# A Fourier filter and a SiLU feed-forward network in one kernel: the first token pairs in two runs, weight rounding moved into the steps, and sums of the inverse transform on GpSimd

## The chip, the cores and the metric

The kernel runs on one core of one Trainium2 chip. The metric is the device time in microseconds (us) of that core; before the change it is 2591.91, the median of 3 runs (2589.95 to 2593.28).

The engines are named as the profile names them: PE is TensorE (matmuls; PEld its weight loads), DVE is VectorE, ACT is ScalarE, POOL is GpSimd, SP is SyncE, which here only issues DMAs. A name with a q (SPq) is an engine's instruction queue.

## What is computed

Two stages follow each other. The first filters every channel of a sequence in the frequency domain; the second is a two-layer network on every token:

```python
# x: (8, 3008, 256); filt_r, filt_i: (1505, 256)
X = np.fft.rfft(x, axis=1)
Y = X * (filt_r + 1j * filt_i)[None]
y = np.fft.irfft(Y, n=3008, axis=1).astype(np.float32)
# 8 * 3008 = 24064 tokens of 256; w_in: (256, 2048), w_out: (2048, 256), both float64
t = y.reshape(24064, 256)
h = t @ w_in
g = h * (1.0 / (1.0 + np.exp(-h)))
out = (g @ w_out).astype(np.float32)
```

## The kernel before

**The transform.** 3008 = 47 x 64, so a transform is done in matmuls with small tables. Stage 1 (tiles `pa`) works along one factor, `forward` (`pb`, L433) along the other. `multiply` (L455) takes the products with the filter, `z` with its real and `p` with its imaginary part. `add` (L463) sums them to a complex product. The inverse is in two parts: `pc` (L476, or L498 for batch 0), whose rows are written to a scratch tensor `d` in HBM, and stage 3 (`pd`, L547), which reads them back as `t4` tiles. Its result is evicted to `y`, half a batch at a time. The 24 slots of frequencies are handled in six groups.

**Batch 0 has a path of its own,** since nothing can hide it: `load_first`, `stage1_first`, `inverse_first`, `rows_first`. `inverse_first` of groups 0 and 1 (`by_gpsimd`) multiplies the sums that GpSimd made. For groups 2 to 5 no sums are made: PE takes twice as many matmuls, with negated tables `neg`. Stage 1 of batch 0 writes into `w_t`, the place where the weights lie later. The transforms of batches 1 to 7 are cut into pieces that lie between FFN matmuls.

**The FFN.** Weights and tokens are cut in 2 x 2, and each product is made with 7 instead of 8 block products (Winograd's form of Strassen's scheme). A *pair* is a set of 2 x 256 tokens (2 x 240 for each third one) of half a batch; there are 48 pairs. A *step* is one pair with one of NJP = 8 pairs of weight blocks: `hidden` has seven matmuls into `px` and `pyz` (L689), sums of them on DVE, SiLU on ACT and four differences on DVE; `project` (L752) has seven matmuls into the accumulators `acc`, one step later. A step has 8 rounds, in which these two and the other pieces take turns. After the eight steps of a pair, `drain` copies the accumulators to `s`, GpSimd makes seven sums and `output` transposes and stores. There is one `s` buffer and one buffer for each accumulator. `tokens` makes the three sums of tokens that a pair needs (`ty`).

**The weights.** They are float64, 16 blocks (j = 0 to 15). A block is rounded to float32 from its two 32-bit words. In `split_weights`, DVE takes exponent and mantissa apart (L877, L880) and ACT converts them (L879, L881). In `round_weights`, DVE adds the low word (L893), limits the exponent (L895) and puts the sign in (L899). In `place_weights` (L908) mantissa and exponent are multiplied into `w_t`. `combine_weights` makes the sums that the scheme needs, for two blocks together. Before the change blocks 0 to 8 are rounded ahead of the FFN, 9 to 15 one a step in steps 0 to 6, where a block's split and rounding stand at one place (round 1) and its placing at round 5.

**Order.** The schedule is written by hand: every engine executes in the order in which the program names the instructions, and semaphores do the rest. Pieces in the FFN are put at a step and a round with `put`. `idle(n)` are matmuls without a use ahead of a stretch of work. DMA issues of SP and ACT stand in their engines' order: an issue that waits holds up all that is behind it.

Of the kernel before, what the change touches and what calls it, by code (L numbers as in the profile page):

```python
# [56 lines left out]
NS, NG = 24, 6  # L57
# [110 lines left out]
def kernel(  # L168
# [96 lines left out]
    def spectral(b):  # L265
# [12 lines left out]
        def load_first():  # L278


            view = w_t.rearrange("p j c w n -> p (j c w n)")
            for at, n0, n in ((view[:, 0:3072], 0, 12), (view[:, 3072:6144], 12, 12),
                              (x_all.rearrange("p i a n -> p (i a n)"), 24, 8)):
                nc.sync.dma_start(out=at, in_=bass.AP(tensor=x.tensor, offset=x.offset + n0 * C,
                                                      ap=[[32 * C, 128], [1, n * C]]))
            xs[0] = view[:, 0:6144].rearrange("p (n c) -> p n c", c=C)
            xs[1] = x_all.rearrange("p i a n -> p (i a n)").rearrange("p (n c) -> p n c", c=C)
            us["t2"] = view[:, 6144:14336].rearrange("p (s c) -> p s c", c=C)
            return view

        def stage1_first(k, i):

            if i == 0:
                banks[k] = bank(b, f"pa_{b}_{k}").rearrange("p a c -> p (a c)").rearrange(
                    "p (n c) -> p n c", c=16)
            n0, n = ((0, 24), (24, 8))[i]
            nc.tensor.matmul(out=banks[k][:, n0:n0 + n], lhsT=wx_t, rhs=xs[i][0:96, :, 16 * k:16 * k + 16],
                             start=True, stop=True)
            if i == 1:
                nc.vector.transpose(out=us["t2"][:, :, 16 * k:16 * k + 16].rearrange("p s c -> p c s"),  # L300
                                    in_=banks.pop(k).rearrange("p n c -> p c n"))
# [139 lines left out]
        def multiply(g, k):  # L441
            if b == 0 and g == NG - 1:

                room = raws["first"].bitcast(FP32).rearrange("p (k i r c) -> p k i r c", k=2, i=2, r=2)
                z, pt = room[:, k, 0], room[:, k, 1]
            else:
                z = zpool.tile([128, 2, C], FP32, name=f"z_{b}_{g}_{k}", tag="z")
            if b == 0 and g == NG - 1:
                pass
            elif b == 0 and k == 1:  # L450
                pt = abcpool.tile([128, 3, C], FP32, name=f"p_{b}_{g}_{k}", tag="abc")[:, 0:2]
            else:
                pt = ppool.tile([128, 2, C], FP32, name=f"p_{b}_{g}_{k}", tag="p")
# [6 lines left out]
        def add(g, k):  # L460
            z, pt = prods[g][k]
            eng = nc.vector if b > 0 else nc.gpsimd
# [19 lines left out]
        def inverse_first(g):  # L482
# [3 lines left out]
            pairs = prods.pop(g)  # L486
            halves[g] = ps
            for h in range(2):
                table = e_t[:, g] if h == 0 else minus[g // 4][:, g % 4]
                terms = [(table[:, :, 0], 0, 0), (table[:, :, 1], 0, 1)]  # L490
                if g not in by_gpsimd:
                    terms += [(table[:, :, 1], 1, 0), (neg[h][:, g], 1, 1)]
                for t, (lhs, which, ri) in enumerate(terms):
                    for i in range(2):
                        rows = slice(64 * i, 64 * i + 64)
                        for k in range(2):

                            nc.tensor.matmul(out=ps[i][64 * k:64 * k + 64, h, :], lhsT=lhs[rows, k],  # L498
                                             rhs=pairs[k][which][rows, ri, :], start=(h == 0 and t == 0),
                                             stop=(t == len(terms) - 1), skip_group_check=True)  # L500

        def rows_first(g):
            for i, pool, tag in ((0, qpool, "q"), (1, opool, "o")):
                qt = pool.tile([128, 2, C], FP32, name=f"q_{b}_{g}_{i}", tag=tag)
                nc.scalar.copy(out=qt, in_=halves[g][i])
                a0 = 8 * g + 4 * i
                queue = nc.gpsimd if g == NG - 2 else nc.scalar
                queue.dma_start(out=d2[a0:a0 + 4].rearrange("a n h c -> (a n) h c"), in_=qt)
# [17 lines left out]
        def load_t4(g, first=0, last=2 * NS):  # L526
# [4 lines left out]
            for h in range(2):  # L531
                queue = nc.scalar if first == 32 and h == 1 else nc.sync
# [125 lines left out]

    def combine(eng, out, in0, in1, op):
# [6 lines left out]
    def tokens(pair):  # L666

        n, yt = pairs[pair][3], channels(pair)
        t = typool.tile([128, 4, CH], FP32, name=f"ty_{pair}", tag="ty")
# [4 lines left out]
        ty[pair] = t  # L674

    def hidden(step):

        pair, jp = divmod(step, NJP)
        n, yt, t = pairs[pair][3], channels(pair), ty[pair]
# [55 lines left out]
    def project(step):  # L735

        pair, jp = divmod(step, NJP)
        n, g = pairs[pair][3], g_t.pop(step)
        if jp == 0:
            acc[pair] = {}  # L740
        last = jp == NJP - 1

        order = PROJECT
        if jp == 0 and step in joined:
            order = PROJECT[0:2] + PROJECT[3:5] + PROJECT[2:3] + PROJECT[5:]
        elif jp == 0:
            order = PROJECT[2:3] + PROJECT[0:2] + PROJECT[3:]
        for c, k, i, h in order:
            if i not in acc[pair]:
                acc[pair][i] = accps.tile([128, 2, 256], FP32, name=f"acc_{pair}_{i}", tag=f"a{i}")  # L750

            nc.tensor.matmul(out=acc[pair][i][:, h, 0:n], lhsT=w_t[:, jp, c, 1], rhs=g[:, k, 0:n],  # L752
                             start=(jp == 0 and h == 0), stop=last, skip_group_check=True)
            if last and (h == 1 or i == 3):
                drain(pair, i)
            yield

    results = {}

    def drain(pair, i):  # L760
        n = pairs[pair][3]

        if i == 0:
            results[pair] = spool.tile([128, 8, CH], FP32, name=f"s_{pair}", tag="s")
# [3 lines left out]
        if pair == len(pairs) - 1:  # L768
            return drain_last(pair, i, n, s, acc[pair])
        copy = v.tensor_copy if i % 2 else nc.scalar.copy  # L770
        if i < 3:
            copy(out=s[:, 2 * i:2 * i + 2, 0:n], in_=acc[pair][i][:, :, 0:n])  # L772
            return
        copy(out=s[:, 6, 0:n], in_=acc.pop(pair)[3][:, 0, 0:n])
        for o, a, b in ((2, 0, 2), (5, 0, 5), (3, 5, 3), (6, 3, 6), (0, 5, 1), (4, 0, 4), (1, 3, 1)):
            combine(gp, s[:, o, 0:n], s[:, a, 0:n], s[:, b, 0:n], ALU.add)
# [20 lines left out]
    def output(pair, chunk):  # L797
# [3 lines left out]
        for h in range(2):  # L801
            v.transpose(out=o[:, :, h, :], in_=results[pair][:, ((2, 6), (4, 1))[chunk][h], :])
# [34 lines left out]
    def load_weights(j):  # L837

        if j in (8, 11, 12, 13):
            pool, tag = (t4pool, "t4") if j in (11, 12) else (upool, "u")  # L840
            raw = pool.tile([128, 2, 512], U32, name=f"raw_{j}", tag=tag)
        else:

            if j in (0, 2):
                t = ypool.tile([128, 2, HALF], FP32, name=f"raw_{j}", tag="y")
                raws.setdefault("tiles", []).append(t)
                raws["at"] = t.rearrange("p a n -> p (a n)").bitcast(U32)[:, 0:2048]
                raws["y"] = raws["at"]
                raws.setdefault("first", raws["at"])
            elif j == 4:  # L850
                raws["at"] = spool.tile([128, 2048], U32, name=f"raw_{j}", tag="s")
            elif j == 6:
                raws["at"] = gpool.tile([128, 2048], U32, name=f"raw_{j}", tag="g")
            elif j in (9, 14):
                raws["at"] = raws["y"]
            at = 1024 * (j in (1, 3, 5, 7, 10, 15))
# [7 lines left out]
    def split_weights(*js):  # L864

        for j in js:
            words = raws[j].rearrange("p w (n t) -> p (w n) t", t=2)
            if j < 8:
                if "scratch" not in raws:
                    raws["scratch"] = gpool.tile([128, 4, 512], U32, name="scratch", tag="g")  # L870
                e, m = (raws["scratch"][:, 2 * (j % 2) + i] for i in range(2))
            else:
                e = zpool.tile([128, 512], U32, name=f"e_{j}", tag="z")
                m = ppool.tile([128, 512], U32, name=f"m_{j}", tag="p")
            raws[j] = lo, hi, e, m, ef, mf = (words[:, :, 0], words[:, :, 1], e, m, e.bitcast(FP32),
                                              m.bitcast(FP32))
# [263 lines left out]
```

## Time and profile before

| | |
|---|---|
| time | 2591.91 us |
| span of the profile | 2589.2 us |
| first FFN matmul | 80.54 us |
| second step begins | 89.35 us |
| mean TensorE clock | 0.996 of full |

A line of a timeline has the start, the length, the engine, the source line, the operation, output <- inputs, shapes and the count; in brackets is the idle time before it and what ended it. A line of a table by stretches has the stretch, its length, then the busy time (and count) of PE, PEld, DVE, ACT and POOL, the granted clock of PE (1.00 is full), the share of the DMA engines and GB/s. On the page, section 1 has busy time, share and instructions of each engine, and section 4 the shares of the chain of waits that ended last. Instructions overlap in an engine's pipeline, so that a distance from start to start is often shorter than a length.

### The profile page before, as it was taken

To read this page: it belongs to the slowest core of one execution; us is meant where nothing else is said; L and a number is where in the kernel's file an instruction comes from. 1 tells how busy PE (TensorE), PEld (TensorE's weight loads), DVE (VectorE), ACT (ScalarE), POOL (GpSimd) and SP (SyncE) were. 2 spreads that over 40 slices of the span, in tenths; PEclk is the share of its full clock that TensorE was granted. 3 is DMA by queue.
4 is the path that set the end of the run, shared out by engine and by line. 5 is a ranking of instruction groups with operands and counts; after the bars stand their busy time and mean duration, and the time that the engine had idled before them with its cause. 6 is when DMAs were issued, how large, how long until landed. Compare 5 with 4: busy or idle time off the path is not lost.

```text
span 2589.2 us, 48332 instructions
## 1 busy us (share of the span) xinstructions
PE 2567.9 (99%) x18972; PEld 2196.3 (85%) x18972; DVE 1691.3 (65%) x3569; ACT 1106.9 (43%) x3014; POOL 426.4 (16%) x672
## 2 busy tenths in 40 slices
PE   8999999999999999999999999999999999999998
PEld 6788888888888888888888888888888888888987
DVE  7766666666666766666666676666666676555554
ACT  3544444444444444443444434444444444444443
POOL 2211211121112111211122111211121112101101
PEclk9899999999999999999999999999999999999999
DMA  8431232222222222222223222231233211210000
GB/s 281 145 82 48 65 80 70 60 61 74 62 63 60 77 66 55 72 68 67 62 62 88 54 66 58 79 72 54 64 75 74 63 47 27 59 25 15 9 17 16
DMA packets 200076, 171.07 MB, mean 66 GB/s; under 512 B 122116, under 2 KB 174196, under 8 KB 199060
## 3 DMA queue, kind: packets, MB, share of 16 engines
q1 hardware_dynamic: 178520, 117.04, 18.7%
q0 software_dynamic: 16928, 44.65, 5.3%
q10 hardware_dynamic: 4400, 6.29, 0.8%
q8 instruction: 149, 2.44, 0.4%
q14 instruction: 79, 0.65, 0.1%
HBM read 96.05 MB, written 81.26 MB: 68 GB/s over the span
## 4 chain that ended last, share of the span: by engine, by line
PE 95%; DVE 1%; DMA 1%; ACT 1%; issue 0%; SPq 0%; ACTq 0%; DVEq 0%
PE acc L752 43%; PE px L689 26%; PE pyz L689 19%; PE pd L547 3%; PE pb L433 2%; PE pc L476 2%; PE pf L403 1%; PE pa L340 0%; DMA w_t<-in_x_dram 0%; DVE g L660 0%; PE pa L331 0%; DMA filt<-in_filt_i_dram 0%; ACT t L344 0%; DMA e_t<-e_tbl 0%; DVE w_t L660 0%
## 5 line engine op out<-in xcount | busy, mean ns | idle before, releaser
L752 PE MATMUL acc<-g,w_t 128*128 128x256 f32 (+1 forms) x5376 | 1512.0, 375 | 0.4 <-DVE g L660 0.4
L752 PEld LDWEIGHTS acc<-g,w_t 128*128 128x128 f32 x5376 | 1021.3, 190 | 115.7 <-DVE g L660 0.8
L660 DVE TENSOR_TENSOR g<-pyz,abc 128x256 f32<-128x256 f32 (+1 forms) x1152 | 479.7, 416 | 563.0 <-ACT abc L710 325.0
L660 DVE TENSOR_TENSOR g<-g 128x256 f32<-128x256 f32 (+3 forms) x1152 | 609.9, 529 | 196.9 <-ACT g L693 183.7
L689 PE MATMUL px<-ty,w_t 128*128 128x256 f32 (+1 forms) x2304 | 684.4, 379 | 0.5 <-ACT abc L710 0.5
L693 ACT ACTIVATE g<-g 128x256 f32<-128x256 f32 (+1 forms) x1152 | 472.9, 410 | 246.7 <-DVE g L660 246.7
L689 PEld LDWEIGHTS px<-ty,w_t 128*128 128x128 f32 x2304 | 426.3, 190 | 82.3 <-issue 26.6
L660 POOL TENSOR_TENSOR s<-s 128x256 f32<-128x256 f32 (+1 forms) x329 | 257.1, 799 | 1439.1 <-DVE s L772 1377.4
L689 PE MATMUL pyz<-y,w_t 128*128 128x256 f32 (+1 forms) x1536 | 452.9, 377 | 0.0
L689 PEld LDWEIGHTS pyz<-y,w_t 128*128 128x128 f32 x1536 | 284.3, 189 | 44.8 <-DVE g L660 5.0
L704 ACT COPY abc<-px 128x256 f32<-128x256 f32 (+1 forms) x384 | 141.5, 368 | 361.3 <-PE px L689 361.3
L710 ACT COPY abc<-px 128x256 f32<-128x256 f32 (+1 forms) x384 | 143.1, 373 | 323.7 <-PE px L689 323.7
L693 ACT ACTIVATE g<-px 128x256 f32<-128x256 f32 (+1 forms) x384 | 146.1, 381 | 308.6 <-PE px L689 308.6
L689 PE MATMUL px<-y,w_t 128*128 128x256 f32 (+1 forms) x768 | 230.2, 381 | 1.1 <-ACT y L246 1.0
L689 PE MATMUL pyz<-ty,w_t 128*128 128x256 f32 (+1 forms) x768 | 225.7, 376 | 0.2 <-DVE g L660 0.2
L689 PEld LDWEIGHTS px<-y,w_t 128*128 128x128 f32 x768 | 141.9, 189 | 23.6 <-issue 5.9
L689 PEld LDWEIGHTS pyz<-ty,w_t 128*128 128x128 f32 x768 | 145.9, 190 | 17.4 <-DVE g L660 1.0
L697 ACT COPY abc<-px 128x256 f32<-128x256 f32 (+1 forms) x384 | 135.5, 353 | 19.5 <-PE px L689 19.5
L547 PEld LDWEIGHTS pd<-wi_t,t 48*64 48x64 f32 x4096 | 69.3, 139 | 32.0 <-ACT g L693 16.4
L547 PE MATMUL pd<-wi_t,t 48*64 48x47 f32 x4096 | 77.2, 238 | 2.3 <-DMA t<-d 1.9
L415 POOL DMA_DIRECT2D d<-tf x144 | 71.4, 503 | 24.0 <-DVE tf L411 20.4
L772 ACT COPY s<-acc 128x512 f32<-128x512 f32 (+1 forms) x94 | 54.3, 578 | 47.5 <-PE acc L752 47.5
(114 smaller groups left out, 1309.1 us busy)
## 6 DMA issues: line engine op xcount, KB each, us to landing
t<-d SPq DMA_DIRECT2D x120, 192.0 KB
d<-q POOLq DMA_DIRECT2D x86, 256.0 KB, 2.6
t<-d SPq DMA_DIRECT2D x84, 256.0 KB
out_dram<-o SPq DMA_DIRECT2D x636, 32.0 KB
d<-tf POOLq DMA_DIRECT2D x144, 96.0 KB, 3.0
xr<-in_x_dram SPq DMA_DIRECT2D x6, 1472.0 KB
x_all<-in_x_dram SPq DMA_DIRECT2D x72, 96.0 KB
x_all<-xr SPq DMA_DIRECT2D x72, 96.0 KB
```

Of the source, the lines that this page charges most:

```text
L415: nc.gpsimd.dma_start(out=d1[k // 2, :, k % 2, n0:n0 + 4], in_=us["tf"][32 * k:32 * k + NS].rearrange("p q n c -> p (q n) c"))
L433: nc.tensor.matmul(out=ps[k][32 * j:32 * j + 32, ri, :], lhsT=d_t[rows, 4 * g + at, ri, :], rhs=t2[rows, at, :], start=True, stop=True)
L476: nc.tensor.matmul(out=ps[j][64 * k:64 * k + 64, a, :], lhsT=e_t[rows, g + a, k, ri, :], rhs=zs[k][rows, ri, :], start=(a == 0 and ri == 0 ...
L547: nc.tensor.matmul(out=ps[h][c0:c0 + 64, cb, i, :], lhsT=t4s[g][rows, i, 128 * cb + c0:128 * cb + c0 + 64], rhs=wi_t[rows, :], start=True, ...
L660: eng.tensor_tensor(out=out, in0=in0, in1=in1, op=op)
L689: nc.tensor.matmul(out=out, lhsT=w_t[:, jp, c, 0], rhs=rhs, start=start, stop=True, skip_group_check=True)
L693: nc.scalar.activation(out=g[:, k, 0:n], in_=g[:, k, 0:n] if src is None else src, func=AFT.Silu)
L697: nc.scalar.copy(out=sums[:, 0, 0:n], in_=xo)
L704: nc.scalar.copy(out=sums[:, 1, 0:n], in_=xo)
L710: nc.scalar.copy(out=sums[:, 2, 0:n], in_=xo)
L752: nc.tensor.matmul(out=acc[pair][i][:, h, 0:n], lhsT=w_t[:, jp, c, 1], rhs=g[:, k, 0:n], start=(jp == 0 and h == 0), stop=last, skip_group ...
L772: copy(out=s[:, 2 * i:2 * i + 2, 0:n], in_=acc[pair][i][:, :, 0:n])
```

## The change

It shortens what has to be done ahead of the first FFN step. Only four weight blocks (0 to 3) are rounded there. The first three pairs are therefore taken in two runs each: pair 0 with weight pairs 0 and 1, then pairs 1 and 2 with weight pairs 0 to 3, then the rest of all three. So new weight pairs are needed in steps 4, 5 and 12 to 15. The sums of a first run are kept (`partial`, in `upool` and in parts of `x_all`), and GpSimd adds them to those of the second. Blocks 4 to 15 are rounded in steps 0 to 3 and 5 to 12, with the four parts of a rounding in rounds 1, 2, 4 and 5 and the placing in round 6.

In the prologue, x comes in 96 instead of 128 partitions, with three matmuls for each transpose. All six groups have their products summed, by GpSimd, or by DVE for the second half of groups 4 and 5; the matmuls with `neg` go. The last eviction of `rows_first` is on DVE, ahead of which nothing else is left. ACT issues the last reads of two slabs instead of half of all.

```diff
-                nc.sync.dma_start(out=at, in_=bass.AP(tensor=x.tensor, offset=x.offset + n0 * C,
-                                                      ap=[[32 * C, 128], [1, n * C]]))
+                nc.sync.dma_start(out=at[0:96], in_=bass.AP(tensor=x.tensor, offset=x.offset + n0 * C,
+                                                            ap=[[32 * C, 96], [1, n * C]]))
...
         def multiply(g, k):
-            if b == 0 and g == NG - 1:
-                room = raws["first"].bitcast(FP32).rearrange("p (k i r c) -> p k i r c", k=2, i=2, r=2)
-                z, pt = room[:, k, 0], room[:, k, 1]
+            if b == 0 and g in (2, 3):
+                if "room" not in us:
+                    us["room"] = gpool.tile([128, 2, 2, 2, C], FP32, name="room", tag="g")
+                z = us["room"][:, g - 2, k]
...
-            eng = nc.vector if b > 0 else nc.gpsimd
+            eng = nc.vector if b > 0 or (g > 3 and k == 1) else nc.gpsimd
...
-                terms = [(table[:, :, 0], 0, 0), (table[:, :, 1], 0, 1)]
-                if g not in by_gpsimd:
-                    terms += [(table[:, :, 1], 1, 0), (neg[h][:, g], 1, 1)]
...
-                nc.scalar.copy(out=qt, in_=halves[g][i])
+                copy = nc.vector.tensor_copy if (g, i) == (NG - 1, 1) else nc.scalar.copy
+                copy(out=qt, in_=halves[g][i])
...
-                queue = nc.scalar if first == 32 and h == 1 else nc.sync
+                queue = nc.scalar if first == 32 and g > 1 else nc.sync
...
+    runs = [(0, 0, 2), (1, 0, 4), (2, 0, 4), (0, 2, 8), (1, 4, 8), (2, 4, 8)]
+    runs += [(pair, 0, NJP) for pair in range(3, len(pairs))]
+    schedule = [(run, jp) for run, (_, first, end) in enumerate(runs) for jp in range(first, end)]
...
     def drain(run, i):
...
+        kept = partial.pop(pair, None)
+        if end < NJP:
+            room = x_all[:, pair - 1] if pair else upool.tile([128, 2, 512], FP32, name="partial", tag="u")
+            partial[pair] = room.rearrange("p a (i n) -> p (a i) n", n=CH)
         for o, a, b in ((2, 0, 2), (5, 0, 5), (3, 5, 3), (6, 3, 6), (0, 5, 1), (4, 0, 4), (1, 3, 1)):
-            combine(gp, s[:, o, 0:n], s[:, a, 0:n], s[:, b, 0:n], ALU.add)
+            out = s[:, o, 0:n]
+            if end < NJP and o in FINAL:
+                out = partial[pair][:, FINAL.index(o), 0:n]
+            combine(gp, out, s[:, a, 0:n], s[:, b, 0:n], ALU.add)
+        if kept is not None:
+            for k, o in enumerate(FINAL):
+                combine(gp, s[:, o, 0:n], s[:, o, 0:n], kept[:, k, 0:n], ALU.add)
...
-    for g in range(2):
+    def inverse(g):
+        part["inverse_first"](g)
+        part["rows_first"](g)
+
+    for g in range(4):
         part["forward"](g)
     for g in range(NG):
         for k in range(2):
             part["multiply"](g, k)
-        if g in by_gpsimd:
-            for k in range(2):
-                part["add"](g, k)
...
-            split(2, 3)
-            rounded(2, 3)
-            placed(2, 3, eng=gp)
-            combine_weights(1, eng=gp)
...
+            part["add"](g, k)
+        if g == 3:
+            part["forward"](5)
+        if g > 0:
+            inverse(g - 1)
+        if g == 1:
+            part["forward"](4)
+        if g == 3:
             for later in range(4):
                 part["load_t4"](later, 0, 24)
...
-    split(4, 5)
-    combine_weights(0)
...
-    split(6, 7, 8)
...
+    inverse(NG - 1)
     for later in range(4):
+        part["load_t4"](later, 32, 2 * NS)
+    second["load_x"](0)
+    weights(4, 5)
+    second["load_x"](1)
+    for k in range(2):
+        for j in (2, 3):
+            round_weights(j, k)
     combine_weights(0)
+    for k in (2, 3):
+        for j in (2, 3):
+            round_weights(j, k)
+    placed(2, 3)
+    combine_weights(1, eng=gp)
+    weights(6, 7)
+    idle(30)
     for g in range(4):
         part["stage3"](g)
...
-    for j in range(9, NJ):
-        put(j - 9, 1, lambda j=j: (split(j), rounded(j)))
-        put(j - 9, 5, placed, j)
+    for j in range(4, NJ):
+        at = j - 4 if j < 8 else j - 3
+        for k, rnd in enumerate((1, 2, 4, 5)):
+            put(at, rnd, round_weights, j, k)
+        put(at, 6, placed, j)
         if j % 2:
+            for k, rnd in ((0, 3), (1, 5)):
+                put(at + 1, rnd, combine_weights, j // 2, k)
+    for step, *js in ((0, 8, 9), (4, 10, 11, 12, 13), (10, 14), (11, 15)):
+        put(step, 0, weights, *js)
+    joined.update((2, 6, 10, 20))
...
+    begun = ((-2, 1), (0, 5), (4, 5), (8, 5), (14, 5), (18, 5))
+    early_stores = (((18, 1), (18, 5)), ((22, 1), (22, 5)))
```

## The prediction

> **What bounds the kernel now.** I read the shares and the chain of waits first, then the PE timeline of the first 100 us, then the other engines beside it.
>
> ```profile
> PE 2567.9 (99%) x18972; PEld 2196.3 (85%) x18972; DVE 1691.3 (65%) x3569; ACT 1106.9 (43%) x3014; POOL 426.4 (16%) x672
> PE 95%; DVE 1%; DMA 1%; ACT 1%; issue 0%; SPq 0%; ACTq 0%; DVEq 0%
> ```
>
> TensorE (PE) is the bound: 99% busy and 95% of the chain. The change leaves the matmuls of the FFN as they are, so it can only move the moment at which the FFN starts, or put holes into it. The PE timeline shows that moment:
>
> ```profile
> 69.93 0.28 PE L547 MATMUL pd<-wi_t,t 48*64 48x47 f32 x2
> 72.10 6.76 PE L547 MATMUL pd<-wi_t,t 48*64 48x47 f32 x246 [1.89 <-DMA t<-d]
> 79.09 0.47 PE L547 MATMUL pd<-wi_t,t 48*64 48x47 f32 x8 [0.23 <-issue]
> 80.54 1.19 PE L689 MATMUL px<-y,w_t 128*128 128x256 f32 x2 [0.98 <-ACT y L246]
> ```
>
> The first FFN matmul is at 80.54; step 1 begins at 89.35. From there to 2589.2 PE waits for almost nothing. So the prologue, 80.5 us, is what can be won. Why it is so long stands in the VectorE (DVE) and GpSimd (POOL) timelines:
>
> ```profile
> 17.95 14.25 DVE L300 STREAM_TRANSPOSE w_t<-pa 128x512 f32<-128x512 f32 x16 [7.25 <-PE pa L297]
> 34.33 0.69 DVE L455 TENSOR_TENSOR z<-pb,filt 128x512 f32<-128x512 f32 x1 [0.89 <-PE pb L433]
> 35.77 0.73 POOL L463 TENSOR_TENSOR z<-z,p 128x256 f32<-128x256 f32 x1 [34.33 <-DVE p L455]
> 36.46 0.73 POOL L464 TENSOR_TENSOR z<-z,p 128x256 f32<-128x256 f32 x1
> 63.63 0.95 DVE L880 TENSOR_SCALAR scratch<-raw 128x512 uint32<-128x512 uint32 x1
> 63.46 3.44 POOL L660 TENSOR_TENSOR w_t<-w_t 128x256 f32<-128x256 f32 x4 [0.47 <-DVE w_t L908]
> ```
>
> Transposes run every 0.89 us, products of the filter every 0.60, GpSimd adds every 0.69. The weight rounding stands between the products on VectorE. The last two lines show a cost used below: a TENSOR_SCALAR that takes 0.42 us takes 0.95 while GpSimd adds.
>
> After 80.54 the balance of a step is in the table by stretches (PE, PEld, DVE, ACT, POOL busy):
>
> ```profile
> 107.90:115.80 7.90, 7.90 (x33) 5.88 (x32) 6.29 (x16) 4.42 (x11) 1.97 (x4) 1.00 0.36 104
> 143.50:149.60 6.10, 6.10 (x30) 5.22 (x29) 3.99 (x9) 2.90 (x10) 1.97 (x4) 1.00 0.43 109
> ```
>
> A step with a stage-1 piece of batch 1 takes 7.9 us, one without 6.05. VectorE is busy 6.3 us in a step that rounds a weight block. That fits in 7.9. It does not fit in 6.05.
>
> **What the Trainium skill says.** "GPSIMD Engine Reference", Specifications: GpSimd's SBUF interfaces are shared with VectorE and contended by instructions in a two-port mode or with two SBUF inputs. The trace agrees (0.42 to 0.95 above). "TensorE: Matmul & The Clock Gate", Part 1: after an idle window of about 3.4 us PE runs at half rate until it has been busy for a window. The trace shows half clock from 72.3 to 86.2, after a hole of only about 2.2 us; so a smaller hole is enough here. [...] Here loads of x run at 415 to 431 GB/s, and a write of d followed by a read takes 2.4 us (issue 50.36, reader goes on at 52.72) to 4.1 us (63.71 to 67.83).
>
> **Part by part.**
>
> 1. x in 96 instead of 128 partitions: 1 MB less, at 0.42 MB/us 2.5 us. The third piece lands at 15.0 instead of 17.4, so the transposes, and the first product, shift by 2.4: 34.33 becomes 31.9. The filters cannot hold this up: the first part has landed by about 26, the second is issued by 32.5 and is needed 4.8 us after the first product.
>
> 2. Products and sums without rounding between them. Four products a group, 2.4 us: six groups plus two VectorE add pairs of 0.67 end at 31.9 + 14.4 + 1.3 = 47.6. GpSimd: 16 adds for groups 0 to 3 and 4 for groups 4 and 5, from 33.3: 20 x 0.69 = 13.8, so 47.1. They end together at about 48 (VectorE's adds lose a little to GpSimd's). Before, the last products ended at 55.0 and the last inverse at 62.0; PE needs 2.0 us for a summed inverse (41.09 to 43.0), so the last one ends at 50.1. The extra products of unsummed groups (neg tables, two more terms) go.
>
> 3. Eviction and the round trip. The two last copies run on ScalarE and VectorE side by side (0.6), two issues: the last write is issued at about 51.4. SyncE's reads of d are issued 0.43 apart: 16 of them from 48.8 to 55.6, then the last rows of slabs 0 and 1. With 2.7 us to land (69.28 to 72.0 before) stage 3 starts at 58.5. Before it was 72.1.
>
> 4. Blocks 2 and 3 on ScalarE and VectorE. ScalarE's part is queued behind its four reads of d, which wait for the last write: write landed 54 to 55.5, four issues of 0.44, six activations of 0.62: 60. Queued behind it are ScalarE's evictions of y. VectorE then has one multiply-add left, a min, two sign merges and four placements: 0.61 + 0.45 + 1.3 + 1.34 = 3.7, until 63.8, and behind that its three evictions of y, 0.75 each: 66.0. All eight are needed by the first FFN matmul. PE, at half clock, would end stage 3 at 65.5 anyway (7 us as before), so this wait costs 0.5 us. FFN starts at **66.0**, 14.5 earlier. Bounds: 64 (short round trip, clock kept) to 68.
>
> 5. Step 0 took 8.8 us at half clock. I leave it at that; if the 30 idle matmuls keep the clock (they end near 57.0, the hole is 1.5 us), it is up to 2.4 us shorter.
>
> 6. Twelve blocks rounded within steps 0-3 and 5-12, where before seven were in steps 0-6. Start to start on VectorE, from its timeline at 90 to 105 and 144 to 164: FFN 3 x 0.34 + 0.60 + 0.79 = 2.41, plus 0.48 wait for ScalarE in front of the wide subtraction: 2.89. A block: 2 x 0.34 + 0.61 + 0.45 + 0.65 + 0.67 = 3.06. Weight combines of a pair 1.33, token sums 1.52, run end (two copies) 1.03, eviction of y 0.80, filter products 1.20. PE needs 7.9 in steps 0-7, 5.7 in steps 8 and 9 (240 columns, no stage 1), 6.9 in 10, 7.1 in 11 and 12 (stage 3 adds 1.08, forward 1.02). VectorE: step 2 8.3, 3 5.95, 6 7.0, 7 7.3; step 8 3.06 + 2.89 + 1.52 = 7.5; step 9 7.3; step 10 7.8; step 11 8.1; step 12 7.2. Over PE's time: 1.8 + 1.6 + 0.9 + 1.0 + 0.1 = **5.4 us**. Splitting the rounding over the rounds removes its 0.97 us wait for ScalarE per block, which I have left out already.
>
> 7. Three more run ends: seven GpSimd adds each, 5.95 us, mostly in steps 3, 7 and 11. VectorE beside them loses 0.53 us on each of three TENSOR_SCALARs and up to 0.4 on two-input operations, 0 to 2.4 a step. Step 3 has 2 us of slack; 7 and 11 do not: 0 to 4.5, I take 2.2. The extra token sums and copies of steps 0 to 7 lie beside PE's 7.9 us. PE may run ahead of VectorE by about three rounds (3 x 0.43 = 1.3), so the holes are 5.4 + 2.2 - 1.3 = **6.3 us**; bounds 4 and 10. Later final sums (four GpSimd adds more) and the late stores are hidden by PE's work in steps 16 to 24.
>
> 8. Loads of blocks 4 to 15 leave the early DMA queue; each 0.5 MB has at least a step to land: nothing.
>
> Sum: -14.5 + 6.3 = -8.2, so 2591.9 - 8.2 = 2583.7.
>
> **Rivals.**
> A. VectorE keeps up, or the clock stays full. For: the first products of a step do not need the rounding, and PE's gap before stage 3 shrinks. Against: the sums of part 6. Gain 14.5 + 2.4 less 2 us of holes: 2577.
> B. Stage 3 starts later than the arithmetic says, from SyncE's row of reads or ScalarE's queue behind the last write. For: before, ScalarE's reads were issued at 69.28, 5.2 us after its last write of 63.71, behind activations. Against: there is less DMA traffic. FFN at 70, holes 8: gain 2.5, 2589.5.
> C. VectorE's excess becomes PE's bound and the holes bring the half clock back in steps 8 to 12, as the small hole at 70 did. Three windows of 3.4 us at half rate lose 5 us, and the waits of steps 2, 7 and 11 repeat: holes of 20 or more. 2591.9 - 14.5 + 20 = 2597.5, slower. Against: PE would still be busy three quarters of each window there.
>
> **How the numbers follow.** Main 0.60 (2579 to 2588), A 0.17, B 0.14, C 0.09. The bound for a difference is 5.2 us: 2586.7 and 2597.1. Main gives 0.57 faster and 0.03 same, A faster, B splits 0.01 faster and 0.13 same, C 0.09 slower: 0.75, 0.16, 0.09. The range takes in A with 2 us below it and B with 2.5 above it, and leaves out most of C: 2575 to 2592.
>
> **What would show it.** The first FFN matmul near 66 (step 4 of the working is wrong if before 62 or after 70); the transposes starting at 15.5; the last inverse ending near 50; a full or a half clock at 60 to 75. In steps 8 to 12 PE waits for "DVE g" of some microseconds in all, with VectorE over 90% busy in that stretch; TENSOR_SCALARs of 0.9 us in steps 3, 7 and 11. The prediction is wrong if PE waits there for a DMA of raw weights, or for w_t.

## The result and the profile after

The changed kernel takes 2634.66 us (median of 4 runs, 2632.28 to 2635.32) beside 2591.84 for the kernel before on the same chip: a ratio of 1.0165, 95% interval 1.015 to 1.0179. It is slower by 43 us. The forecast was 2583.7, faster by 8. All line numbers below are those of the changed kernel, unless an experiment starts from the kernel before.

On the page of the changed kernel, busy times and chain of waits:

```profile
PE 2570.1 (98%) x18852; PEld 2200.3 (84%) x18852; DVE 1712.5 (65%) x3603; ACT 1104.6 (42%) x3013; POOL 450.8 (17%) x704
PE 93%; DVE 3%; DMA 2%; ACT 1%; issue 0%; SPq 0%; ACTq 0%; DVEq 0%
```

PE still does about 2570 us of work; but the chain that set the end has 3% on DVE and 2% on DMA where it had 1% each. The span went from 2589.2 to 2630.5, so 41.3 us are to be found. PE's timeline at the start of the FFN:

```profile
71.99 7.15 PE L540 MATMUL pd<-wi_t,t 48*64 48x47 f32 x239 [5.40 <-DMA t<-d]
82.48 0.68 PE L540 MATMUL pd<-wi_t,t 48*64 48x47 f32 x17 [3.35 <-issue]
84.15 1.19 PE L689 MATMUL px<-y,w_t 128*128 128x256 f32 x2 [0.98 <-ACT y L246]
```

Stage 3 begins at 71.99, as before the change (72.10), though five blocks fewer are rounded ahead of it, and has a gap of 3.35 us in it. The first FFN matmul is at 84.15 instead of 80.54: **3.6 us of the loss**, where a gain of 14.5 was forecast. From there to the end it is 2546.4 us instead of 2508.7: **37.7 us**. PE's waits from 80 to 320 us show what kind of loss this is (columns: sum, times, longest):

```profile
PE pyz L689 <- DVE g L658: 28.1, 16, 4.9
PE pd L540 <- issue: 3.3, 1, 3.3
...
PE px L689 <- ACT abc L710: 0.5, 1, 0.5
```

Before the change the first of these was 0.2 us. PE's next product into `pyz` waits for DVE's sum `g`, 16 times, up to 4.9 us. The longest is for the last sum of step 2 and holds up step 3. DVE's timeline there, with the PE line that ends the wait:

```profile
109.57 0.42 DVE L658 TENSOR_TENSOR g<-pyz,abc 128x256 f32<-128x256 f32 x1 [1.90 <-ACT abc L710]
109.91 0.68 DVE L775 COPY s<-acc 128x512 f32<-128x512 f32 x1
110.51 0.68 DVE L905 SCALAR_TENSOR_TENSOR m<-raw,m 128x512 f32<-128x512 uint32 x1
111.11 2.13 DVE L907 TENSOR_SCALAR e<-e 128x512 uint32<-128x512 f32 x1
113.16 1.27 DVE L658 TENSOR_TENSOR w_t<-w_t 128x256 f32<-128x256 f32 x2
114.36 0.68 DVE L910 SCALAR_TENSOR_TENSOR e<-raw,e 128x512 uint32<-128x512 uint32 x1
114.96 0.41 DVE L777 COPY s<-acc 128x256 f32<-128x256 f32 x1
115.30 1.27 DVE L919 TENSOR_TENSOR w_t<-m,e 128x256 f32<-128x256 f32 x2
116.49 0.41 DVE L658 TENSOR_TENSOR g<-pyz,abc 128x256 f32<-128x256 f32 x1
...
116.96 1.22 PE L689 MATMUL pyz<-y,w_t 128*128 128x256 f32 x2 [4.94 <-DVE g L658]
```

The first line is the sum of round 4 (call it g2), the last DVE line that of round 7 (g1). `pyz` has one buffer, so PE's next product into it must wait until g1 has read it. Between the two stand, in DVE's fixed order, the last two parts of a rounding (put at rounds 4 and 5), a weight combination (5), a placing (6) and the two copies of a run end: 6.9 us, in a stretch for which PE has 2 us of work. And DVE was idle for 1.90 just before g2. One of the lines, a TENSOR_SCALAR of normally 0.42 us, takes 2.13; GpSimd was making the sums of the run that had ended.

The stretch that follows, and the whole stretch of new steps (columns as in the table by stretches before):

```profile
116.00:126.00 10.00, 9.04 (x27) 6.80 (x28) 5.17 (x11) 4.29 (x11) 4.21 (x7) 0.71 0.11 26
82.00:226.00 144.00, 115.59 (x633) 87.31 (x633) 102.54 (x220) 61.41 (x150) 34.06 (x54) 0.92 0.32 94
```

After the wait the mean granted clock is 0.71 for 10 us. DVE is busy for 71% of the 144 us (102.54), so it is not short of time as a whole.

PE's waits for `g` and `abc` are 28.6 us after the change and 0.7 before, 27.9 of the 37.7 us. A part of the rest is the clock. Its mean is 0.96 in the 265.85 us from 84.15 to 350, against 0.99 in the 239.46 us from 80.54 to 320 before the change; by these rounded means some 8 us more are lost to it (an estimate).

### The profile page after: what moved, and what is told of

Same layout as the page of the kernel before. It is cut to its first block, busy times and chain, and to the rows that moved or that the text cites. A ratio compares the mean times of both kernels' runs of the same rounds, so it can differ in the third digit from the quotient of the medians.

```text
span 2630.5 us, 48184 instructions
## 1 busy us (share of the span) xinstructions
PE 2570.1 (98%) x18852; PEld 2200.3 (84%) x18852; DVE 1712.5 (65%) x3603; ACT 1104.6 (42%) x3013; POOL 450.8 (17%) x704
## 4 chain that ended last, share of the span: by engine, by line
PE 93%; DVE 3%; DMA 2%; ACT 1%; issue 0%; SPq 0%; ACTq 0%; DVEq 0%
PE acc L753 42%; PE px L689 25%; PE pyz L689 18%; PE pd L540 3%; PE pb L430 2%; PE pc L472 2%; PE pf L400 1%; DVE g L658 1%; DMA x_all<-in_x_dram 1%; PE pa L337 0%; PE pa L328 0%; DVE w_t L919 0%; DMA filt<-in_filt_r_dram 0%; DVE e L910 0%; DVE e L907 0%
## 5 line engine op out<-in xcount | busy, mean ns | idle before, releaser
L658 POOL TENSOR_TENSOR s<-s 128x256 f32<-128x256 f32 (+1 forms) x338 | 264.8, 800 | 1448.8 <-DVE s L775 1431.7
L689 PE MATMUL pyz<-y,w_t 128*128 128x256 f32 (+1 forms) x1536 | 455.4, 378 | 28.2 <-DVE g L658 28.1
```

The lines of the kernel that those rows point to most:

```text
L658: eng.tensor_tensor(out=out, in0=in0, in1=in1, op=op)
L689: nc.tensor.matmul(out=out, lhsT=w_t[:, jp, c, 0], rhs=rhs, start=start, stop=True, skip_group_check=True)
```

## The experiments

Theories at this point. **T1, place:** what lies between g2 and g1 makes the waits. **T2, throughput:** DVE has too much work in these steps wherever it stands. **T3, GpSimd:** its additions at the new run ends hold up DVE. **T4, start:** x in 96 partitions is slow. Times of the kernel before ran from 2591.2 to 2591.8 beside all of them.

| run | us | ratio, 95% | first FFN matmul | from there to the end | PE's waits for `g` and `abc` |
|---|---|---|---|---|---|
| before | 2591.8 | | 80.54 | 2508.7 | 0.7 |
| changed | 2634.7 | 1.015 to 1.0179 | 84.15 | 2546.4 | 28.6 |
| x128 | 2632.2 | 1.0137 to 1.0168 | 80.13 | 2545.9 | 28.8 |
| early_rounds | 2617.6 | 1.0086 to 1.0116 | 83.41 | 2532.0 | 17.0 |
| one_place | 2617.2 | 1.0083 to 1.0117 | 82.47 | 2532.2 | 16.2 |
| no_first_sums | 2626.4 | 1.012 to 1.0151 | 83.77 | 2540.7 | 24.5 |
| before_x96 | 2596.2 | 1.0011 to 1.0029 | 85.44 | 2508.4 | 0.7 |
| prologue | 2625.9 | 1.0118 to 1.0149 | 77.88 | 2546.1 | 28.6 |
| spread | 2611.4 | 1.0064 to 1.0094 | 87.42 | 2527.0 | 11.7 |
| both | 2602.5 | 1.0028 to 1.0058 | 76.74 | 2525.4 | 12.0 |
| before_runs | 2612.8 | 1.0067 to 1.0097 | 81.16 | 2528.9 | 11.3 |
| shade | 2599.5 | 1.0021 to 1.0042 | 81.40 | 2519.0 | 7.7 |
| runs_alone | 2605.7 | 1.004 to 1.007 | 82.00 | 2522.5 | 10.7 |
| runs_no_sums | 2598.8 | 1.0017 to 1.0038 | 81.32 | 2516.6 | 6.8 |

The fifth column is the span of the profile less the fourth. The fourth moves by 1 to 4 us between profiles of one prologue (in the profile of spread the second piece of x itself came 2 us later than in that of the changed kernel); the fifth is the steadier one.

### x128: x in 128 partitions again

```diff
-                nc.sync.dma_start(out=at[0:96], in_=bass.AP(tensor=x.tensor, offset=x.offset + n0 * C,
-                                                            ap=[[32 * C, 96], [1, n * C]]))
+                nc.sync.dma_start(out=at, in_=bass.AP(tensor=x.tensor, offset=x.offset + n0 * C,
+                                                            ap=[[32 * C, 128], [1, n * C]]))
```

> The changed kernel with x loaded into 128 partitions again, all else as it is. Theory (96 partitions load slower): the third piece of x lands near 17.4 us instead of 21.3, the first transpose starts near 18 instead of 22.2, the first FFN matmul is near 78 to 80 instead of 84.15, and the time falls by 4 to 6 us to about 2629. Rival (the load was slow for another cause, such as the order of the requests): the third piece still lands at 21 or later, no change.

The tables by stretches from 8 to 14 us, in which x is read, of the changed kernel, of before and of x128:

```profile
8.00:14.00 6.00, 6.00 (x51) 6.00 (x51) 3.60 (x7) 1.43 (x3) 0.00 (x0) 1.00 1.03 240
```

```profile
8.00:14.00 6.00, 5.90 (x53) 5.71 (x52) 2.32 (x4) 1.65 (x3) 0.00 (x0) 1.00 0.98 415
```

```profile
8.00:14.00 6.00, 6.00 (x55) 6.00 (x55) 3.60 (x7) 1.48 (x3) 0.00 (x0) 1.00 1.00 425
```

The DMA engines are full in all three (1.03, 0.98, 1.00), but with 96 partitions they move 240 GB/s instead of 415 to 425. A quarter fewer bytes take longer: the third piece is waited for until 21.33 instead of 18.58. The FFN starts 4.0 us earlier, and nothing changes behind it. In the median the gain (2.5 us) is smaller than in the profile, and the intervals overlap.

### early_rounds and one_place: the parts of a rounding in other rounds

The first edit is early_rounds, the second one_place:

```diff
-        for k, rnd in enumerate((1, 2, 4, 5)):
+        for k, rnd in enumerate((0, 1, 3, 3)):
```

```diff
-        for k, rnd in enumerate((1, 2, 4, 5)):
+        for k, rnd in enumerate((1, 1, 1, 1)):
...
-        put(at, 6, placed, j)
+        put(at, 5, placed, j)
```

> The changed kernel with the four parts of a rounding in rounds 0, 1, 3, 3 instead of 1, 2, 4, 5; placing stays in round 6. Same work, same steps. Theory of position (what stands on VectorE between the sum g2 of round 4 and the sum g1 of round 7 delays g1, for which TensorE's next zo product waits): TensorE's waits for VectorE fall from 28 us to 8 to 14 and the half-clock stretches after the long holes go, so the time falls by 15 to 25 us to about 2615. Rival of throughput (VectorE has too much work in a step): the waits stay above 22 us and the time moves by less than 5.

> The changed kernel with a block's whole rounding in round 1 and its placing in round 5, as it stood before the change, but for the same blocks in the same steps. Theory of position: VectorE waits about 1 us for ScalarE inside each block, yet TensorE's waits fall to 8 to 16 us and the time to about 2617. Rival of throughput: the added wait for ScalarE makes it slower than the changed kernel, 2640 or more.

Both gain 17 us, 14 of them from the first FFN matmul on: the same instructions in the same steps, with a block's rounding ahead of g2 instead of partly behind it. T1 holds, and the part of the change that splits the rounding over the rounds was a loss by itself: one_place has the grouping of the kernel before, and is faster. But 16 to 17 us of waits stay, in other places (8 to 14 and 8 to 16 were expected). In one_place six of them, in steps 7 to 12, are for ScalarE's copy of `px`, like this one:

```profile
167.50 0.61 ACT L899 ACTIVATE m<-m 128x512 f32<-128x512 uint32 x1
168.02 0.34 ACT L704 COPY abc<-px 128x240 f32<-128x240 f32 x1
...
168.41 0.67 PE L689 MATMUL px<-ty,w_t 128*128 128x240 f32 x2 [1.36 <-ACT abc L704]
```

The copy stands behind ScalarE's two conversions of the block. The kernel before has exactly this order in its steps 0 to 6, and no wait, because of what PE does there:

```profile
100.66 1.88 PE L331 MATMUL pa<-x_all,wx_t 96*128 96x512 f32 x4
101.21 0.61 ACT L881 ACTIVATE m<-m 128x512 f32<-128x512 uint32 x1
101.73 0.35 ACT L704 COPY abc<-px 128x256 f32<-128x256 f32 x1
...
102.38 0.60 PE L689 MATMUL px<-ty,w_t 128*128 128x256 f32 x2
```

The stage-1 matmuls of batch 1, 1.88 us in round 3 of steps 0 to 7, cover the delay. Steps 8 and 9 have no such cover. In step 7 of one_place the cover is there and a wait of 1.15 us stays: ScalarE starts late, since DVE's two TENSOR_SCALARs ahead of its conversions take 0.94 and 0.95 beside GpSimd's sums.

### no_first_sums: GpSimd's sums of the first runs left out

```diff
             partial[pair] = room.rearrange("p a (i n) -> p (a i) n", n=CH)
+            gp.memset(partial[pair][:, :, 0:n], 0.0)
+            return
```

> The changed kernel without GpSimd's seven sums of the first runs of pairs 0 to 2 (what they should keep is set to zero, so those three pairs' outputs lack the first runs' part). Theory of contention (GpSimd's sums block VectorE): the operations on VectorE beside them that took 0.9 to 2.1 us take 0.42 again, the three longest holes of TensorE (4.9, 4.4 and 3.1 us) shrink to about 2 us each, and with the half clock after them the time falls by 8 to 14 us. Rival (the copies and combines of these steps make the holes): the holes stay above 3.5 us, the time falls by less than 4.

It gains 8.2 us; the long waits of 4.94, 4.37 and 3.14 us become 3.41, 2.98 and 1.61. So T3 is real, and not the main cause here.

### before_x96, prologue, spread, both

before_x96 is the kernel before with the 96-partition read alone (and one copy that reads the piece over 96 partitions as well). prologue has x128's edit and these:

```diff
-    idle(36)
+    idle(52)
...
-        if g == 3:
-            for later in range(4):
-                part["load_t4"](later, 0, 24)
         if g == 4:
             for later in range(4):
-                part["load_t4"](later, 24, 32)
+                part["load_t4"](later, 0, 32)
...
-    weights(6, 7)
     idle(30)
...
-    for step, *js in ((0, 8, 9), (4, 10, 11, 12, 13), (10, 14), (11, 15)):
-        put(step, 0, weights, *js)
+    for step, rnd, *js in ((0, 5, 6, 7), (2, 0, 8, 9), (4, 0, 10, 11, 12, 13), (10, 0, 14), (11, 0, 15)):
+        put(step, rnd, weights, *js)
```

spread changes the plan of the FFN steps only (weight combinations go to round 3 too, with two of the twelve in round 5), and both is the two together:

```diff
-    for j in range(4, NJ):
-        at = j - 4 if j < 8 else j - 3
-        for k, rnd in enumerate((1, 2, 4, 5)):
+    steps = (0, 1, 2, 3, 4, 5, 6, 7, 8, 10, 11, 12)
+    for j, at in zip(range(4, NJ), steps):
+        for k, rnd in enumerate((1, 2, 3, 3)):
             put(at, rnd, round_weights, j, k)
-        put(at, 6, placed, j)
+        put(at, 5, placed, j)
...
-    begun = ((-2, 1), (0, 5), (4, 5), (8, 5), (14, 5), (18, 5))
+    begun = ((-2, 1), (1, 3), (5, 3), (9, 3), (14, 5), (18, 5))
```

> The kernel before with one edit: its three pieces of x are read into 96 partitions instead of 128, as the changed kernel does. If reading into 96 partitions is itself the slow thing (240 GB/s against 415 to 425), the third piece lands near 21 us here too and everything up to stage 3 moves by some 3 to 4 us: 2595 us. The rival, that the third piece was late in the changed kernel for another reason (what else is in flight at that time), gives the third piece at 17 to 18 us and 2592 us.

> The changed kernel with its FFN plan untouched and four edits ahead of the FFN: x in 128 partitions, 16 more idle products so that the clock is not lost before the third piece, the two sets of reads of d for rows 0 to 31 joined into one (8 reads on SP instead of 16), and the loads of blocks 6 to 9 put in steps 0 and 2 instead of beside stage 3. If the start of the FFN was late for these reasons, the first product moves to about 35, the last read of d lands near 65, the 3 us gap in the middle of stage 3 goes, and the FFN starts at 72 to 74 instead of 80.1 with x in 128 partitions alone: 2622 us with the FFN as long as it was. The rival, that stage 3 is held by the d round trip whatever the number of reads, gives 79 and 2630 us. The gap in stage 3 tells apart its own two causes: if it stays without the loads beside it, the loads did not make it.

> The changed kernel as it is ahead of the FFN, with another plan for the FFN: the parts of a block's rounding in rounds 1, 2, 3 and 3, placing in round 5, blocks 8 to 11 one step earlier (steps 4 to 7, which still have a product of the second batch's stage 1 of 1.9 us in round 3 to cover them), blocks 12 to 15 in steps 8, 10, 11 and 12, combining in round 3 and token sums of the second to fourth run in round 3 of steps 1, 5 and 9, away from the run ends. Theory (what stands between g2 and g1 of one step makes the holes, and a block needs cover): holes fall from 37 us to 5 to 8, time 2600 us. Rival (VectorE's or GpSimd's share alone makes them): the same work in other rounds leaves some 16 us as in the two earlier re-orderings, 2617 us.

> The last two together. If the lost start and the holes add up independently: 2592 us, the time of the kernel before, or a few us less. If stage 3's start and the first steps compete for VectorE (the rounding of blocks 2 and 3 then runs beside stage 3's copies), some 5 us of the start is given back: 2597 us.

**before_x96** confirms T4 with one edit: 240 GB/s again, 2596.2 us, 4.9 us slower (2.9 to 7.5 by the interval). **prologue** gains 8.7 us, and the FFN starts at 77.9; neither the forecast 66 nor the 72 to 74 expected of this run. The gap in stage 3 is shorter than in x128 (2.97 us) but still there (1.72 us; in both, with the same prologue, 2.00), though the loads of blocks 6 to 9 are gone from beside it, so these alone did not make it. **spread** gains 23.3 us and has 11.7 us of waits, none over 1.1, but not the 5 to 8 expected. **both** (2602.5) is 11.2 above the kernel before, and above the two times expected of it, 2592 and 2597.

### before_runs, runs_alone, runs_no_sums: the two-run order by itself

The kernel before with the two-run order of the first three pairs, and nothing else of the change: blocks 0 to 8 stay ahead of the FFN, 9 to 15 in steps 0 to 6.

```diff
+    runs = [(0, 0, 2), (1, 0, 4), (2, 0, 4), (0, 2, 8), (1, 4, 8), (2, 4, 8)]
...
+    begun = ((-2, 1), (1, 3), (5, 3), (9, 3), (14, 5), (18, 5))
```

In before_runs the kept sums of pair 0 lie in a tile of `qpool`, in runs_alone in two of `opool`. runs_no_sums is runs_alone with this ahead of the seven additions of a first run:

```diff
             partial[pair] = rooms
+            for r in rooms:
+                gp.memset(r[:, 0:n], 0.0)
+            return
```

> The kernel before with one part of the change alone: the first three token pairs in two pieces each (the runs, their drains, the kept partial sums, the token sums of the second to fourth run in round 3 of steps 1, 5 and 9), while blocks 0 to 8 stay rounded ahead of the FFN and 9 to 15 in steps 0 to 6. If the pieces cost little by themselves and the twelve blocks are what makes the holes: FFN start 80.5 as before, holes at most 3 us (three more run ends and the additions on GpSimd), 2594 us. Rival: the run ends and GpSimd's additions make a good part of the holes: 8 us of holes, 2602 us.

> The kernel before with the two-piece order alone, as in the run called before_runs, but the kept sums of pair 0 lie in two idle output tiles instead of a tile that the second batch's copies wait for (that wait held PE for 4.1 us at 224.8 us there and belongs to my edit, not to the change). Expected: that hole gone, 2607 to 2608 us, 16 us above the kernel before, from run ends.

> The same without GpSimd's seven additions after the first piece of each of the three pairs (the kept sums are set to zero instead, so that pairs 0 to 2 lack what their first pieces give). If GpSimd's additions, which hold up VectorE's instructions for some 2 us at the run ends (two placing or combining operations took 2.92 and 2.61 us there instead of 0.75), make the long holes: the two holes of 2.8 and 2.6 us go, 2600 us. Rival, that the run end's copies and the token sums on VectorE make them by their place alone: 2606 us.

This was the surprise. runs_alone takes 2605.7: the two-run order costs **14.1 us** with the weight blocks as they were. Its timeline at the end of step 3, DVE and POOL and the PE line at the end:

```profile
108.59 2.92 DVE L935 TENSOR_TENSOR w_t<-m,e 128x256 f32<-128x256 f32 x2
108.94 0.74 POOL L665 TENSOR_TENSOR partial<-s 128x256 f32<-128x256 f32 x1
109.62 1.60 POOL L665 TENSOR_TENSOR s<-s 128x256 f32<-128x256 f32 x2
...
111.76 0.41 DVE L665 TENSOR_TENSOR g<-pyz,abc 128x256 f32<-128x256 f32 x1
...
112.23 1.22 PE L696 MATMUL pyz<-y,w_t 128*128 128x256 f32 x2 [2.80 <-DVE g L665]
```

The placing, two operations that take 0.75 us together when nothing is beside them, takes 2.92 because GpSimd adds; g1 stands behind it. In runs_no_sums the same two lines, with a memset on GpSimd instead:

```profile
107.50 0.75 DVE L938 TENSOR_TENSOR w_t<-m,e 128x256 f32<-128x256 f32 x2
...
108.97 0.70 PE L696 MATMUL pyz<-y,w_t 128*128 128x256 f32 x2 [0.63 <-DVE g L665]
```

2598.8 us: GpSimd's first-run sums cost 6.9 of the 14.1. The other 7 are left when these sums are gone. Ten waits for `g` of at most 1.0 us remain, 5.5 us in all; seven of them (3.5 us) end in steps 1 to 3 and 5 to 7, around the token sums (put at steps 1 and 5) and the run ends' copies (steps 2 and 6), which points to these by their place on DVE. The other three come later, from 198 to 256 us. No run takes them apart. In before_runs the time was 2612.8, above both times expected of it (2594 and 2602); 7.1 us of that was an effect of my own edit (PE waited 4.11 for a copy into a tile of `qpool` that the kept sums still held, and the mean clock was 0.68 in the 5 us behind it).

### shade: two blocks back in the wait for d

both, with blocks 4 and 5 loaded early and rounded while d makes its round trip, all reads of d on SP, 34 more idle products, and ten blocks in steps 0 to 7, 11 and 12. Blocks 6 and 7 are loaded ahead of stage 3 again, 8 and 9 in step 0:

```diff
-    weights(2, 3)
+    weights(2, 3, 4, 5)
-                queue = nc.scalar if first == 32 and g > 1 else nc.sync
+                queue = nc.sync
...
-    idle(30)
+    idle(64)
```

> The kernel called both, with blocks 4 and 5 rounded ahead of the FFN after all, in the time in which VectorE waits for d's round trip (58 to 66 us): their loads go out right behind those of blocks 2 and 3, all reads of d go to SP so that ScalarE's part of the rounding no longer stands behind them, 34 more idle products keep the clock up to stage 3, and ten blocks are left in steps 0 to 7, 11 and 12. If the holes come from blocks without cover and the half clock in stage 3 from PE's idling: FFN start at 73 to 75 instead of 76.7, holes 5 to 6 us instead of 12, 2590 to 2593 us. Rival, that stage 3's start is set by the round trip and its copies now wait for VectorE: FFN start 78, 2598 us.

The waits fall to 7.7 us, not quite to the 5 to 6 expected; but the FFN starts at 81.40, 4.7 us later than in both. The time is near the rival's 2598, but its reason is not in the trace:

```profile
56.99 14.56 PE L967 MATMUL idle<-wx_t 96*128 96x128 f32 x128
71.48 2.30 PE L540 MATMUL pd<-wi_t,t 48*64 48x47 f32 x140
77.09 3.44 PE L540 MATMUL pd<-wi_t,t 48*64 48x47 f32 x116 [3.31 <-issue]
```

PE goes from its 64 idle products straight to stage 3, without a wait for d. SP had issued its last read of d by 67.30, and DVE's first copy of y waits 2.14 us for PE, not PE for DVE. So at the end it was my own 34 more idle products that held stage 3 back; at 0.23 us each they take 7.7 us. They kept the clock at full for its first 140 matmuls. Whether fewer would win a part of the 4.7 us back, no run shows. In all 2599.5, the best of the versions made from the changed kernel, and still 1.0031 (1.0021 to 1.0042) of the kernel before. No version beat the kernel before.

## Why the prediction was wrong

Both terms of the sum failed. The start was to come 14.5 us earlier (parts 1 to 4) and came 3.6 later; the holes were to cost 6.3 us (parts 6 and 7), and from the first FFN matmul on 37.7 were lost.

**Part 1 (x in 96 partitions), wrong.** It took bytes over a rate measured with 128 partitions: third piece at 15.0. PE's wait for it ended at 21.33, since the rate fell with the partitions. The Trainium skill, "SBUF — State Buffer", section "Door 1: The DMA port swizzle (why `[64,N]` ≈ `[32,N]`)", would have warned: partitions 0 to 63 are reached by the even half of the ports only, 64 to 127 by the odd half. With 96, two thirds of the bytes go over half of the ports; an estimate from the page's 218 GB/s for that half is 327 GB/s. The runs show 240, which the page does not explain, and the measurement decides. In the wait the clock also fell (0.50 from 20 to 26 us): the first transposes came 1.7 us apart instead of 0.89. The first product was at 39.58 instead of 31.9.

**Part 2 (products and sums), nearly right.** First product to last inverse was to take 18.2 us and took 20.1 (39.58 to 59.7). The two extra microseconds are a wait of DVE for a DMA (1.45, at a product with the filter, though part 1 had said that the filters cannot hold this up; the trace names `wi_t`, issued behind them) and one of DVE's adds beside GpSimd (0.95 instead of 0.41).

**Part 3 (round trip of d), wrong by 3.9 us.** From the last inverse to stage 3, 8.4 us were forecast and 12.3 passed (59.7 to 71.99). The reads were not issued 0.43 apart: SP's 20 reads took 13.7 us, 0.69 each. The trace before could have warned: there SP's last 12 reads took 7.43 us, 0.62 each. SP's waits in the changed kernel:

```profile
SPq L526 <- DMA d<-q: 14.9, 3, 13.7
SPq L526 <- DMA t<-d: 5.8, 6, 2.0
```

In the first line the longest, 13.7, lies ahead of the row, so that 1.2 us of it fall within. The second line is what I had not counted: waits of reads of d that the trace puts down to earlier reads of d, six times. Why they wait is not shown. Rival B named this row of reads, but with a start at 70.

**Part 4 (stage 3 to the FFN), wrong by 4.7.** 7.5 us were forecast and 12.2 passed, with 3.35 of them in the gap that is put down to "issue" (more on it in the last section). ScalarE's part of blocks 2 and 3 did stand behind its reads, as said; it held nothing up, since the copies of y came later still. PE at half clock from 72 on was foreseen, and right. The four differences, 7.7 at the first product, 1.9, 3.9 and 4.7, add up to the 18.2 between 66.0 and 84.15.

**Part 6 (twelve blocks in the steps), wrong in kind.** It compared DVE's sum of work with PE's time, step by step, and found 5.4 us too much, all of it in steps 8 to 12 (by its own numbers step 2 was 0.4 over as well, 8.3 against 7.9, and is not in the sum). The trace has DVE busy for 71%, and for 78% in steps 8 to 12 (36.81 us of 47.10), where over 90% was to show it; and 14.3 of the 28.1 us of waits for `g` fall ahead of step 8. What counts is the order: in a step DVE has two deadlines, and the work must fit between them. So the failing step is this comparison of sums, and with it the sentence "Splitting the rounding over the rounds removes its 0.97 us wait for ScalarE per block", which counts the split as a gain: the split took the last two parts from before g2 and put them between g2 and g1. early_rounds and one_place gave 17 us back by that alone. The place of the blocks is another part of the same error: part 6 did give steps 8 and 9 less time, but a step without stage-1 work also has nothing to cover ScalarE's part.

**Part 7 (run ends), wrong in size.** Forecast 2.2 us for GpSimd, bounds 0 to 4.5, "up to 0.4 on two-input operations". Measured: 6.9 us by runs_alone against runs_no_sums, 8.2 in the changed kernel; one pair of two-input operations lost 2.17 us. Copies and token sums, which I called hidden by 7.9 us of PE's work, are what is left for another 7. And "PE may run ahead by about three rounds" is too much with one `pyz` buffer: behind the product that g1 reads (at 110.56) PE makes two more, 0.9 us, and stops at the next into `pyz`. The Trainium skill says it more sharply than I used it: "SBUF — State Buffer", section "SBUF: two separate sides", has the shared ports held for a whole instruction while the other engine fully waits. For an instruction with two SBUF inputs the page says so only against a GpSimd instruction that reads SBUF. The 2.92 beside 0.74 and 1.60 on GpSimd agrees with that, and so does the 0.75 beside a memset.

**The sum by runs.** Of 43 us: 14 with the two-run order (runs_alone); 3.6 with the later start, in the profile; 25 are left over. I put these down to the twelve blocks, by subtraction: no run has the blocks without the runs, and runs_alone has its token sums in other rounds than the changed kernel. Better places give 17 to 23 back (early_rounds, spread, which moves the token sums too). Rival C came nearest: holes over 20 and the half clock after them, but from order and not from DVE's excess, and not only in steps 8 to 12; and it kept the gain of 14.5 at the start, which was not there. T2, throughput, is not needed for the long waits; whether it makes the last 8 to 12 us of waits in shade and both is open.

## What to carry to other kernels

When work is moved beside a bound engine, don't compare sums of busy time: write down, for the helping engine's fixed order, between which two deadlines each piece lands and how much of the bound engine's work lies between them. What was hidden in its old place (here by 1.88 us of stage 1) has to be costed anew in the place it moves to. And a start that is computed from unloaded rates needs each link measured: partitions, waits among the reads, and the clock that idling costs.

## What the runs showed of the hardware

- A read into 96 partitions moved 240 GB/s with the DMA engines full, against 415 to 425 into 128, in two kernels (the changed one and before_x96).
- A TENSOR_SCALAR of 0.42 us took 2.13, and two TENSOR_TENSORs of 0.75 took 2.92, beside GpSimd additions of 0.7 to 0.8 us each; beside a GpSimd memset they took 0.75.
- Whether the clock fell after a wait of PE did not follow from the length of the wait. In no_first_sums it stayed at 1.00 after 3.41 us and fell to 0.50 after 2.34. After 2.34 in the changed kernel and 2.39 in early_rounds it stayed at 1.00, after 2.38 in one_place it fell. Before the change it fell at 72.7, after 1.89 at stage 3, and came back at 86.3. So the prediction's "a smaller hole is enough here" holds for that place and is no rule.
- A gap in PE's row of stage-3 matmuls, put down to "issue", stands in every run: 0.23 us before the change, 3.35 in the changed kernel, 3.52 at most (no_first_sums). In the changed kernel 17 matmuls of stage 3 come after it; with 16 more idle products ahead 48 do (both, 2.00 us), with 34 more than that 116 (shade, 3.31 us). So it belongs to a place in PE's row of instructions. Its end goes with a transfer of 0.02 MB on a DMA queue of the kind "instruction" (q8): in all fourteen runs the gap ends 2.4 to 3.0 us after the start of one, whether that lies ahead of the gap (71.5 in both, end at 74.24) or inside it (79.8 in the changed kernel, end at 82.48). That PE waits there for its next instructions is the likely reading. No run tested it, nor what sets the time of the transfer.
